# Strided q and k of two batches loaded in 96 rows of three pieces, batch 0's outputs placed behind its scores, and batch 1 in the order of the later batches

## The chip, the cores and the metric

The kernel runs on one core of one Trainium2 chip. The metric is the time of one execution on the device in microseconds (us); the figure that is compared is the median of several runs. A single profiled execution of each kernel supplies the spans, the waits and the order of the work.

## What is computed

Attention with two kinds of sparse mask over 8 batches, 8 heads, 576 positions and a head size of 64, then a two-layer block with a squared ReLU over the 4608 token rows. Heads 0 to 3 are *local* (a query sees itself and the 31 positions before it), heads 4 to 7 are *strided* (a query sees the earlier positions that are equal to it modulo 32).

```
scores = scale * q @ k.T                       # per batch and head
local:   0 <= i - j < 32
strided: i >= j and i % 32 == j % 32
attn = softmax(where(mask, scores, -1e9)); o = attn @ v
x = o.transpose(0, 2, 1, 3).reshape(4608, 512)
g = relu(x @ w_in) ** 2                        # 512 -> 2048
out = g @ w_out                                # 2048 -> 512
```

## The kernel before, in words

**Units.** A unit `u` is a pair of heads of one batch, four to a batch: units 0 and 1 of batch 0 are local, 2 and 3 strided, units 4 to 7 are batch 1, and so on. A unit goes through steps that are written as functions:

- T (`step_T`, L268 to L292): turns q or k so that the head size lies on the partitions. TensorE transposes slice by slice into one PSUM bank (L276) and ScalarE (L289) or VectorE (L291) copies 128x576 to SBUF. A local q or k takes six transposes of 96 rows, a strided one eight of 72 rows.
- S (`step_S`, L297 to L359): the scores, four half-tiles in four PSUM banks, one for each head of the pair and each half of the positions, matmuls at L325. For batch 0 a matmul (L313) first puts a mask bias in the bank; for later batches a mask is multiplied in afterwards by VectorE (L341). ScalarE takes the exponential of each bank (L335). With `at_once` the four exponentials stand together; otherwise they are spread over the next groups of the second stage (L354 to L359).
- N and O (`step_N`, `step_O`): only for the strided units of batch 0; row sums with a matrix of ones (L373), their inverse as exp(-ln) on ScalarE (L375, L376), the product with v (L386) and the scaling (L388).
- D (`step_D`): for all other units, attention times v in two or three parts (L410), each with a reciprocal and a multiplication on VectorE (L422, L423).
- E (`step_E`): the result is turned back (L440) and copied into `xt`, the input of the second stage (L446, L448).

**Second stage.** It walks over nine chunks of 512 rows. `mm1` (L464) makes one of 16 column blocks (`ff`) of the hidden layer with four matmuls of 512 columns, ScalarE applies ReLU (L470), VectorE squares (L473). `mm2` (L487) multiplies with `w_out`. These calls stand in a list of *groups*; attention steps are hooked in front of chosen groups. For batch 0, `first_steps` (L512 on) writes the order out by hand; beside each step stands the number of idle matmuls (`warm`, L502 to L506) that follow it. For batch 1 the calls of `second` (L731 to L748) name the group of each step; later batches come from `stream_steps` and are spread by weights.

**PSUM.** Eight banks: two `ph`, one `py`, five `pt`, each list taken in rotation. While `mm2` of chunk 0 runs, its fourth output holds one of the five `pt` banks.

**Queues.** Loads with a cast to bf16 are issued by GpSimd (POOL) in the order of the program: strided q and k of batch 0 (L226), local unit 1 (L130), v of batch 0, four parts of `w_in`, the first part of `w_out`, then in `loads_1` batch 1 mixed with the rest of `w_out`. The first local unit and, from batch 2 on, q, k and v come through SyncE (SP); the first of those waits for the last part of `w_out` (L117). TensorE, VectorE and ScalarE each run their instructions in the program's order.

**The strided loads.** `load_str_first` brings batch 0's strided q and k as 72 rows with 4 heads x 512 elements each into room in `w_out_b`; `load_qk_str` brings batch 1's unit by unit, again in 72 rows. From batch 2 on strided q and k are cast to DRAM and turned by the DMA queue, which leaves both strided units of a batch in one tile of 288 columns; `step_S` reads that layout where the batch is 2 or more (L322).

Of the kernel before, what the change touches and what calls it, by code (L numbers as in the profile page):

```python
# [14 lines left out]
def kernel(  # L15
# [125 lines left out]
                 s[name + "f"].rearrange("p h (j d) -> p h j d", j=6))  # L141
            s[name] = t

    def load_qk_str(u):
        b, p = units[u]
        s = st.setdefault(u, {})
        for name, src in (("q", q), ("k", k)):
            t = strT.tile([128, NJ // 2, 4 * SP_], BF16, name=f"{name}T_s")
            t = t.rearrange("p a c -> p (a c)")[0:SP_, 0:2 * NJ * D].rearrange("p (h c) -> p h c", h=2)
            nc.gpsimd.dma_start(out=t, in_=src[b, 2 * p:2 * p + 2]  # L150
                                .rearrange("h (p j) d -> p h (j d)", j=NJ))
            s[name] = t

    XB = 2
    big = {}
# [9 lines left out]
    def transpose_str(b):  # L165
        for name in "qk":
            o = strT.tile([128, NJ // 2, 4 * SP_], BF16, name=f"{name}T_s")
            nc.sync.dma_start_transpose(out=o, in_=big.pop((b, name)))
            for i in range(2):
                st.setdefault(4 * b + 2 + i, {})[name + "T"] = o[:, :, 2 * SP_ * i:2 * SP_ * (i + 1)]  # L170

    def transpose_local(u):
        s = st[u]
# [44 lines left out]
        for u in range(2):  # L218
            st.setdefault(4 * b + u, {})["v"] = vls[i + u]

    def load_str_first(names):
        for i, (name, src) in enumerate((("q", q), ("k", k))):
            if name not in names:
                continue
            t = w_out_b[0:SP_, 4 * i + 4:4 * i + 8, :]
            nc.gpsimd.dma_start(out=t, in_=src[0, 4:8].rearrange("h (p j) d -> p h (j d)", j=NJ))  # L226
            for u in (2, 3):
                st.setdefault(u, {})[name] = t[:, 2 * (u - 2):2 * (u - 1)]

    def load_v_str(u, eng):  # L230
        b, p = units[u]
        t = v_st.tile([SP_, 2, NJ * D], FP32, name="v_st")
# [35 lines left out]
    def step_T(u, name):  # L268
        s = st[u]
        local = is_local(u)  # L270
        n, w = (6, QL) if local else (NJ, SP_)
        src = s[name]
        src = src.rearrange("p j h d -> p (j h d)" if local else "p h c -> p (h c)")
        pt = bank("ph" if u < 4 else "pt").bitcast(BF16)[:, 0:S]
        for j in range(n):
            nc.tensor.transpose(pt[:, w * j:w * (j + 1)], src[:, 128 * j:128 * (j + 1)],  # L276
                                ident[0:w, 0:w])
        if local and name == "k":
            full = kTl[v_slot(u)]
            dst = full[:, 32:32 + S]  # L280
        else:
            full = dst = qkT.tile([128, S], BF16, name=f"{name}T")
        if local:
            o = dst.rearrange("c (p j) -> c p j", j=6)
            i = pt.rearrange("c (j p) -> c p j", j=6)
        else:
            o, i = dst, pt
        if name == "q" and (u > 3 or u == 0):
            nc.scalar.copy(o, i)  # L289
        else:  # L290
            nc.vector.tensor_copy(o, i)  # L291
        s[name + "T"] = full  # L292
# [4 lines left out]
    def step_S(u, at_once=False):  # L297
        s = st[u]
        qT, kT = s["qT"], s["kT"]
        local = is_local(u)  # L300
        w, n = (QL, NL) if local else (SP_, NJ)
        kn = 128 if local else SP_
        hn = n // 2
        e = es[u % 4]
        s["e"] = e
        pss = [[None, None], [None, None]]
        for half in range(2):
            for row in range(2):
                pss[row][half] = bank("pt")
                if u < 4:  # L310
                    bias = bias_l[:, half].rearrange("p t c -> p (t c)") if local \
                        else bias_s.rearrange("p t c -> p (t c)")
                    nc.tensor.matmul(pss[row][half][0:kn, 0:S // 2], ident[0:kn, 0:kn], bias,  # L313
                                     start=True, stop=False, skip_group_check=True)
            for i in range(hn):
                t = half * hn + i
                klo = w * t
                for row in range(2):
                    rows = slice(64 * row, 64 * row + 64)
                    if not local and units[u][0] >= XB:  # L320
                        c0 = w * (t // 4)
                        lhsT, rhs = (a[rows, t % 4, c0:c0 + w] for a in (kT, qT))  # L322
                    else:
                        lhsT, rhs = kT[rows, klo:klo + kn], qT[rows, w * t:w * (t + 1)]
                    nc.tensor.matmul(pss[row][half][0:kn, w * i:w * (i + 1)], lhsT, rhs,  # L325
                                     start=u > 3, stop=True, skip_group_check=u < 4)

        for row in range(2):
            for half in range(2):
                unread[id(pss[row][half])] = u  # L330

        def expo(row, half):
            del unread[id(pss[row][half])]
            lo = S * row + S // 2 * half
            nc.scalar.activation(e[0:kn, lo:lo + S // 2], pss[row][half][0:kn, 0:S // 2],  # L335
                                 AF.Exp, scale=scale)

        def masks(row):
            x = e[0:kn, S * row:S * (row + 1)].rearrange("p (t c) -> p t c", c=w)
            m = mask_full if local else mask_str.to_broadcast([kn, n, w])  # L340
            nc.vector.tensor_tensor(x, x, m, op=ALU.mult)  # L341

        if u < 4:
            for half in range(2):
                for row in range(2):
                    expo(row, half)
            return
        if at_once:
            for row in range(2):
                for half in range(2):  # L350
                    expo(row, half)
            later(1, lambda: masks(0), u)
            later(2, lambda: masks(1), u)
            return  # L354
        expo(0, 0)
        later(1, lambda: expo(0, 1), u)
        later(2, lambda: (masks(0), expo(1, 0)), u)
        later(3, lambda: expo(1, 1), u)
        later(4, lambda: masks(1), u)  # L359
# [146 lines left out]
                nc.tensor.matmul(pw, idle[:, 0:128], idle, start=True, stop=True)  # L506

    idle = xt[0][:, T - 512:T]
    first_order = (0, 2, 3, 1)
    NP = 5  # L510

    def first_steps():  # L512
# [3 lines left out]
        def part(kks, ffs=range(NP)):  # L516
            for ff in ffs:
                mm1(0, ff, kks, first_order, None if ff < 2 else "py" if ff == 2 else "pt")

        cast1 = lambda nm: (lambda: cast_qk_local(1, (nc.vector.tensor_copy,) * 2, nm))  # L520
        order = [(t(0, "q"), 2), (t(0, "k"), 3), (S_(0), 0), (t(2, "q"), 0), (t(2, "k"), 1), (S_(2), 0),
                 (t(3, "q"), 0), (t(3, "k"), 1), (cast1("q"), 0), (cast1("k"), 0), (S_(3), 0),
                 (t(1, "q"), 0), (t(1, "k"), 1), (D_(0, 0), 0), (D_(0, 1), 0), (n(2), 1), (S_(1), 1),
                 (o(2), 0), (E_(0), 0), (n(3), 0), (D_(1, 0), 0), (D_(1, 1), 0), (o(3), 0), (lambda: part((a, b)), 0),
                 (E_(1), 0), (lambda: part((c,)), 0), (lambda: part((d,)), 0)]
        return order

    def has_T(u):
        return units[u][0] < (LB if is_local(u) else XB)

    def stream_steps(lo, hi, base):
        order = [T_(lo, "q"), T_(lo, "k"), T_(lo + 1, "q"), S_(lo), T_(lo + 1, "k")]
# [22 lines left out]
    def loads_1():  # L555
        load_qk_local_sw(1, (4, 5), "q")
        load_qk_local_sw(1, (4, 5), "k")
        load_w_out(1)
        load_v_local_sw(1)
        load_qk_str(6)  # L560
        load_qk_str(7)
        load_v_str_sw(1)
        load_w_out(2)
        load_w_out(3)
        for t in vl_sts:
            nc.gpsimd.memset(t[0:32], 0.0)

    def loads(b):
# [6 lines left out]
        load_v_str(u + 3, nc.sync)  # L575
        if b >= XB:
            cast_str_dram(b)
        if b < XB:
            load_qk_str(u + 2)
        cast_qk_local(u, pool2)  # L580
        cast_qk_local(u + 1, pool2)
        if b < XB:
            load_qk_str(u + 3)
        cast_v_local(u)
        cast_v_local(u + 1)
        cast_v_str(u + 2)
# [18 lines left out]

    nc.scalar.preload_act_table_set("natural_log_exp_and_others")
    load_qk_local(0, nc.sync)
    load_str_first("qk")
    make_identity(nc, ident)
    nc.vector.memset(idle, 0.0)  # L610
    nc.vector.memset(mask_loc, 1.0)
# [45 lines left out]
    for fn, spare in first:  # L657
        fn()
        warm(spare)
        tick()  # L660
    late_constants()
    loads_1()

    NCH = T // 512
# [64 lines left out]

    dve2 = (nc.vector.tensor_copy,) * 2  # L730
    second(12, lambda: cast_qk_local(4, dve2))  # L731
    second(13, T_(4, "q"))
    second(14, T_(4, "k"), lambda: cast_qk_local(5, dve2))
    second(15, T_(5, "q"))
    second(16, S_(4, True), T_(5, "k"))
    second(18, S_(5, True))
    second(19, D_(4, 0), T_(6, "q"))
    second(20, D_(4, 1), T_(6, "k"), lambda: cast_v_str(6, nc.scalar.copy))
    second(21, S_(6, True), T_(7, "q"))
    second(22, E_(4), D_(5, 0), T_(7, "k"), lambda: cast_v_str(7, nc.scalar.copy))  # L740
    second(23, D_(5, 1), S_(7, True))
    second(24, D_(6, 0))
    second(25, E_(5), D_(6, 1))
    second(26, D_(6, 2))
    second(27, D_(7, 0))
    second(28, D_(7, 1), E_(6))
    second(29, D_(7, 2))
    second(31, E_(7))  # L748
    plan(2, 18, 0, 0)
    done_prev, g_prev = 0, 32  # L750
    plan(3, 34, 0, 0)
# [49 lines left out]
```

## Time and profile before

| | us |
|---|---|
| five runs | 324.71, 325.84, 319.21, 320.25, 321.17 |
| their median | 321.17 |
| the profiled execution | 324.71 |
| its span, first to last instruction | 322.7 |
| TensorE busy in the span | 303.5 |
| VectorE, ScalarE, GpSimd busy | 166.6, 163.9, 84.6 |

The profiled execution is near the top of the five. "PEclk" is the clock that was granted to TensorE, 1.00 being full speed; "idle before" is time that an engine sat still just before an instruction, with what ended it. TensorE carries the kernel: from 121 us to 305 us, 180.5 of 184 us are busy. Batch 0 takes the time from the start to about 30 us, batch 1 that from 38 us to 64.5 us; the first matmul of the second chunk starts at 64.53.

### The profile page before, as it was taken

The page shows a single profiled execution, that of the slowest core. Times are in us where ns is not written, and L with a number is a line of the kernel's source. Part 1 is how long each engine was busy: PE and PEld are TensorE (multiplying, and loading weights), DVE is VectorE, ACT ScalarE, POOL GpSimd, SP SyncE. Part 2 cuts the span into 40 slices and gives each one's busy share as a digit, 9 for nine tenths or more (in the row PEclk, how much of TensorE's full clock was granted, in tenths as well). Part 3 has the DMA queues.
Part 4 walks back from the last instruction along what each step waited for, and adds up shares of the span by engine and source line. Part 5 has one row for each costly group of instructions (what it writes and reads, how often), then busy time and mean ns, then how long its engine had stood idle before and what let it go on. Part 6 is the DMA issues. An engine that isn't in the chain of part 4 may idle for free.

```text
span 322.7 us, 6155 instructions
## 1 busy us (share of the span) xinstructions
PE 303.5 (94%) x2342; PEld 150.7 (47%) x2386; DVE 166.6 (52%) x408; ACT 163.9 (51%) x335; POOL 84.6 (26%) x108
## 2 busy tenths in 40 slices
PE   8699988999899998999999999999999999999995
PEld 3454445554455454444444444444454444444442
DVE  4444565547965786757575656565466222222200
ACT  3454666477554764554555455545553434434311
POOL 8542313714940623713084006000000000000000
PEclk9958999999999999999999999999999999999999
DMA  7999988899999998998699666000110110000121
GB/s 140 156 203 205 176 147 228 195 164 283 197 203 185 218 220 193 221 192 195 163 240 158 143 143 145 35 32 35 51 53 32 39 60 35 32 32 35 41 89 65
DMA packets 87949, 43.41 MB, mean 135 GB/s; under 512 B 72497, under 2 KB 81393, under 8 KB 87729
## 3 DMA queue, kind: packets, MB, share of 16 engines
q1 hardware_dynamic: 73520, 31.86, 42.7%
q0 software_dynamic: 14400, 11.17, 25.2%
q8 instruction: 18, 0.29, 0.4%
q14 instruction: 11, 0.08, 0.1%
HBM read 37.08 MB, written 12.98 MB: 155 GB/s over the span
## 4 chain that ended last, share of the span: by engine, by line
PE 84%; DVE 5%; DMA 3%; ACT 3%; issue 2%; POOL 2%; ACTq 0%; DVEq 0%; POOLq 0%
PE ph L464 35%; PE py L487 26%; PE ph L487 9%; PE pt L410 4%; PE pt L325 3%; DMA vl<-in_v_dram 3%; ACT r L470 2%; PE pt L440 2%; PE pt L276 1%; DVE xt L448 1%; PE pt L487 1%; DVE g_sb L473 1%; DVE x_l L423 1%; DVE e L341 1%; DVE kTl L291 1%
## 5 line engine op out<-in xcount | busy, mean ns | idle before, releaser
L464 PE MATMUL ph<-xt,w_in_b 128*128 128x512 bf16 x549 | 142.0, 380 | 3.4 <-DVE xt L448 1.9
L470 ACT ACTIVATE r<-ph 128x512 bf16<-128x512 f32 x141 | 84.0, 598 | 98.6 <-PE ph L464 94.1
L473 DVE TENSOR_TENSOR g_sb<-r 128x512 bf16<-128x512 bf16 x144 | 68.5, 478 | 109.2 <-ACT r L470 108.4
L487 PE MATMUL py<-w_out_b,g_sb 128*128 128x512 bf16 x381 | 99.9, 379 | 1.4 <-issue 0.5
L487 PEld LDWEIGHTS <-g_sb 128*128 128x128 bf16 x576 | 52.9, 98 | 60.0 <-issue 3.1
L464 PEld LDWEIGHTS <-w_in_b 128*128 128x128 bf16 x576 | 51.9, 98 | 54.8 <-issue 2.2
L335 ACT ACTIVATE e<-pt 128x288 bf16<-128x288 f32 (+1 forms) x128 | 48.3, 407 | 15.9 <-PE pt L325 15.7
L487 PE MATMUL ph<-w_out_b,g_sb 128*128 128x512 bf16 x152 | 37.1, 379 | 0.4
L410 PEld LDWEIGHTS <-e 72*128 72x128 bf16 (+1 forms) x416 | 22.4, 99 | 19.3 <-issue 2.7
L199 POOL CAST vl<-vl_st 128x768 bf16<-128x768 f32 x12 | 10.9, 911 | 49.6 <-DMA vl_st<-in_v_dram 42.6
L423 DVE TENSOR_TENSOR x_s<-pt,rinv 72x384 bf16<-72x384 f32 (+1 forms) x42 | 21.4, 509 | 1.4
L341 DVE TENSOR_TENSOR e<-e,mask_str 72x576 bf16<-72x576 bf16 x28 | 17.4, 621 | 3.9 <-ACT e L335 3.9
L140 POOL CAST q_l<-q_st 96x768 bf16<-96x768 f32 x12 | 11.8, 985 | 25.6 <-DMA q_st<-in_q_dram 13.8
L423 DVE TENSOR_TENSOR x_l<-pt,rinv 96x384 bf16<-96x384 f32 x32 | 17.7, 554 | 1.1
L422 DVE RECIPROCAL rinv<-pt 96x6 f32<-96x6 f32 (+2 forms) x74 | 13.6, 184 | 8.3 <-PE pt L410 8.1
L491 ACT COPY y<-py 128x512 f32<-128x512 f32 x25 | 14.7, 586 | 4.2 <-PE py L487 4.2
L410 PE MATMUL pt<-vs,e 72*128 72x65 bf16 x224 | 13.9, 193 | 1.2 <-ACT e L335 1.1
L341 DVE TENSOR_TENSOR e<-e,mask_full 128x576 bf16<-128x576 bf16 x28 | 14.2, 508 | 1.0 <-ACT e L335 1.0
L491 ACT COPY y<-ph 128x512 f32<-128x512 f32 x10 | 5.9, 586 | 17.0 <-PE ph L487 17.0
L140 POOL CAST k_l<-k_st 96x768 bf16<-96x768 f32 x12 | 11.0, 919 | 12.2 <-DMA k_st<-in_k_dram 12.1
L410 PE MATMUL pt<-vl,e 128*128 128x65 bf16 x192 | 11.3, 199 | 1.9 <-DMA vl<-in_v_dram 1.9
L240 POOL CAST vs<-v_st 72x1024 bf16<-72x1024 f32 x12 | 12.9, 1100 | 0.4
(101 smaller groups left out, 170.9 us busy)
## 6 DMA issues: line engine op xcount, KB each, us to landing
out_dram<-y SPq DMA_DIRECT2D x36, 256.0 KB, 2.0
vl_st<-in_v_dram SPq DMA_DIRECT2D x24, 144.0 KB, 4.0
v_st<-in_v_dram SPq DMA_DIRECT2D x12, 288.0 KB
q_st<-in_q_dram SPq DMA_DIRECT2D x16, 144.0 KB, 8.2
k_st<-in_k_dram SPq DMA_DIRECT2D x16, 144.0 KB, 5.7
w_in_b<-in_moe_w_in_dram POOLq DMA_DIRECT2D x4, 512.0 KB, 14.1
w_out_b<-in_moe_w_out_dram POOLq DMA_DIRECT2D x4, 512.0 KB, 13.3
q_d<-in_q_dram POOLq DMA_DIRECT2D x6, 288.0 KB, 5.1
```

The costliest lines, as they stand in the source:

```text
L140: copy(t.rearrange("p j h d -> p h j d"), s[name + "f"].rearrange("p h (j d) -> p h j d", j=6))
L240: (copy or nc.gpsimd.tensor_copy)(t[:, :, 0:D], s["vf"].rearrange("p h (j d) -> p (h j) d", d=D))
L335: nc.scalar.activation(e[0:kn, lo:lo + S // 2], pss[row][half][0:kn, 0:S // 2], AF.Exp, scale=scale)
L341: nc.vector.tensor_tensor(x, x, m, op=ALU.mult)
L410: nc.tensor.matmul(po[:, n - n0, :], e[0:kn, pos(n):pos(n) + 128], rhs[0:kn, src(n), 0:D + 1], start=True, stop=True)
L422: nc.vector.reciprocal(rinv[0:w, 0:m], po[0:w, 0:m, D:D + 1])
L423: nc.vector.tensor_tensor(x, po[0:w, 0:m, 0:D], rinv[0:w, 0:m].to_broadcast([w, m, D]), op=ALU.mult)
L464: nc.tensor.matmul(ph, w_in_b[:, kk, 128 * ff:128 * (ff + 1)], xt[kk][:, 512 * c:512 * (c + 1)], start=(kk == order[0]), stop=(kk == order ...
L470: nc.scalar.activation(r, ph, AF.Relu)
L473: later(1, lambda: nc.vector.tensor_tensor(g[:, ff, :], r, r, op=ALU.mult))
L487: nc.tensor.matmul(py, g[:, ff, 128 * j:128 * (j + 1)], w_out_b[:, ff, :], start=(ff == 0), stop=(ff == 15))
L491: nc.scalar.copy(y, py)
```

## The change

Five edits:

1. `load_str_first` and the old `load_qk_str` give way to one `load_qk_str` for batches 0 and 1. It brings the four strided heads as 288 rows of 512 elements, laid out as 96 partitions with 3 pieces; batch 0 into `w_out_b`, batch 1 into a `qk_st` buffer instead of `strT`.
2. `step_TS` turns them: for q or k two halves, each of six transposes of 96 rows into one bank, then one 128x576 copy, into the layout that the later batches use. `step_S` reads that layout for every strided unit.
3. Batch 0's order: both strided q halves ahead of the first scores, all scores ahead of row sums and outputs, other numbers of idle matmuls (ten after the first eight before, nineteen now), `late_constants` moved up onto VectorE behind the first k copy, and `mm1` taking the four parts of `xt` in their natural order.
4. Batch 1's order: a list in the manner of `stream_steps`, spread over groups 13 to 30; the scores of units 5 to 7 stay `at_once`, those of unit 4 do not.
5. `loads_1` has one call, two DMAs, where four DMAs stood.

```diff
-    def load_qk_str(u):
...
-            nc.gpsimd.dma_start(out=t, in_=src[b, 2 * p:2 * p + 2]
-                                .rearrange("h (p j) d -> p h (j d)", j=NJ))
+    def load_qk_str(b, names="qk", room=None):
...
+            if room is None:
+                t = qk_st.tile([QL, 2, 6 * D], FP32, name=f"{name}_st")
+                t = t.rearrange("p h c -> p (h c)").bitcast(BF16).rearrange("p (c x) -> p c x", c=3)
+            else:
+                t = room[0:QL, 3 * i:3 * i + 3, :]
+            nc.gpsimd.dma_start(out=t, in_=src[b, 4:8].rearrange("h (p j) d -> (h p) (j d)", j=NJ)
+                                .rearrange("(c r) x -> r c x", r=QL))
+            big[b, name] = t
...
+    def step_TS(b, name, half, copy):
+        if half == 0:
+            o = strT.tile([128, NJ // 2, 4 * SP_], BF16, name=f"{name}T_s")
+            for i in range(2):
+                st.setdefault(4 * b + 2 + i, {})[name + "T"] = o[:, :, 2 * SP_ * i:2 * SP_ * (i + 1)]
+            big[b, name + "T"] = o
+        src = big[b, name]
+        pt = bank("ph" if b == 0 else "pt").bitcast(BF16)[:, 0:S]
+        for j in range(2):
+            for c in range(3):
+                lo = 128 * (2 * half + j)
+                nc.tensor.transpose(pt[:, 3 * QL * j + QL * c:3 * QL * j + QL * (c + 1)],
+                                    src[:, c, lo:lo + 128], ident[0:QL, 0:QL])
+        copy(big[b, name + "T"][:, 2 * half:2 * half + 2, :].rearrange("c j p -> c (j p)"), pt)
...
-                    if not local and units[u][0] >= XB:
+                    if not local:
...
-    first_order = (0, 2, 3, 1)
+    first_order = (0, 1, 2, 3)
...
-        order = [(t(0, "q"), 2), (t(0, "k"), 3), (S_(0), 0), (t(2, "q"), 0), (t(2, "k"), 1), (S_(2), 0),
-                 (t(3, "q"), 0), (t(3, "k"), 1), (cast1("q"), 0), (cast1("k"), 0), (S_(3), 0),
-                 (t(1, "q"), 0), (t(1, "k"), 1), (D_(0, 0), 0), (D_(0, 1), 0), (n(2), 1), (S_(1), 1),
-                 (o(2), 0), (E_(0), 0), (n(3), 0), (D_(1, 0), 0), (D_(1, 1), 0), (o(3), 0), (lambda: part((a, b)), 0),
-                 (E_(1), 0), (lambda: part((c,)), 0), (lambda: part((d,)), 0)]
+        order = [(t(0, "q"), 2), (t(0, "k"), 0), (late_constants, 0), (ts("q", 0, s_), 0), (ts("q", 1, v_), 1), (S_(0), 1),
+                 (ts("k", 0, v_), 0), (ts("k", 1, v_), 2), (cast1("q"), 0), (cast1("k"), 0), (S_(2), 1),
+                 (t(1, "q"), 0), (t(1, "k"), 1), (S_(3), 3), (S_(1), 3), (n(2), 1), (n(3), 1),
+                 (D_(0, 0), 0), (D_(0, 1), 0), (D_(1, 0), 0), (D_(1, 1), 0), (o(2), 2), (E_(0), 1),
+                 (E_(1), 0), (o(3), 0), (lambda: part((a, b)), 0), (lambda: part((c,)), 0), (lambda: part((d,)), 0)]
...
-        load_qk_str(6)
-        load_qk_str(7)
+        load_qk_str(1)
...
-    second(13, T_(4, "q"))
-    second(14, T_(4, "k"), lambda: cast_qk_local(5, dve2))
-    second(15, T_(5, "q"))
-    second(16, S_(4, True), T_(5, "k"))
-    second(18, S_(5, True))
...
+    second(13, lambda: cast_qk_local(5, dve2))
+    second(22, lambda: cast_v_str(6, nc.scalar.copy))
+    second(24, lambda: cast_v_str(7, nc.scalar.copy))
+    ts = lambda nm, half: (lambda: step_TS(1, nm, half, nc.scalar.copy if nm == "q" else nc.vector.tensor_copy))
+    batch1 = [T_(4, "q"), T_(4, "k"), T_(5, "q"), S_(4), T_(5, "k"), S_(5, True), D_(4, 0), ts("q", 0), D_(4, 1),
+              ts("q", 1), ts("k", 0), D_(5, 0), ts("k", 1), E_(4), D_(5, 1), S_(6, True), E_(5), S_(7, True),
+              *D_all(6), D_(7, 0), E_(6), D_(7, 1), D_(7, 2), E_(7)]
+    for i, step in enumerate(batch1):
+        second(13 + i * 37 // (2 * len(batch1)), step)
```

## The prediction, made before the changed kernel was run

> **What bounds the kernel now.** I read the page's chain first, then the waits of TensorE in the part that the change touches, then the windows and the timeline of that part.
>
> The chain that ended last, by engine (page, part 4):
>
> ```profile
> PE 84%; DVE 5%; DMA 3%; ACT 3%; issue 2%; POOL 2%; ACTq 0%; DVEq 0%; POOLq 0%
> ```
>
> TensorE is the chain. Other engines count only where TensorE waits for them, so I price what the change does to TensorE's own work and to its waits before 64.53 us, where chunk 1 starts. Behind that point the order of all engines is the same in both kernels, PSUM bank numbers apart, and 180.5 of the 184 us from 121 to 305 are TensorE work: what is won or lost ahead of 64.53 moves the end one for one.
>
> TensorE's waits from 0 to 65 us (us in total, times, longest):
>
> ```profile
> PE pt L410 <- DMA vl<-in_v_dram: 1.9, 2, 1.4
> PE pt L276 <- DVE q_l L140: 1.7, 2, 1.2
> PE ph L276 <- DMA w_out_b<-in_k_dram: 1.4, 1, 1.4
> ...
> PE pt L325 <- DVE x_l L423: 0.7, 1, 0.7
> ```
>
> The change aims at these: v (1.9) and the strided k (1.4) in batch 0, q's cast (1.7) in batch 1. But a larger item is no wait. Windows (stretch, its length, busy us and instructions of PE, PEld, DVE, ACT, POOL, then clock, DMA share, GB/s):
>
> ```profile
> 6.09:9.50 3.41, 2.62 (x34) 1.38 (x32) 1.22 (x2) 1.50 (x5) 3.41 (x5) 1.00 1.22 175
> 9.50:12.92 3.42, 2.69 (x47) 1.84 (x48) 0.95 (x3) 1.33 (x4) 2.75 (x4) 1.00 2.19 165
> 12.92:16.33 3.41, 1.79 (x33) 1.19 (x33) 2.28 (x5) 1.33 (x4) 0.00 (x0) 1.00 1.77 134
> 16.33:19.74 3.41, 2.98 (x26) 1.44 (x27) 1.40 (x4) 1.40 (x3) 2.10 (x3) 0.50 1.23 201
> 19.74:23.15 3.41, 3.41 (x39) 1.71 (x40) 1.19 (x2) 2.11 (x6) 1.47 (x2) 0.50 1.24 207
> 23.15:26.57 3.42, 3.09 (x33) 1.87 (x33) 2.50 (x6) 1.25 (x3) 1.17 (x2) 0.50 1.24 206
> ```
>
> After a stretch with 1.79 us of TensorE work the clock is 0.50 for 10.24 us; stretches with 2.62 and 2.69 did not lower it.
>
> The timeline of TensorE around it (start, us, engine, line, operation):
>
> ```profile
> 6.18 0.42 PE L276 MATMUL ph<-ident,k_l 96*128 96x96 bf16 x6
> 6.44 0.81 PE L506 MATMUL py<-xt 128*128 128x512 bf16 x3
> 7.09 0.41 PE L313 MATMUL pt<-w_out_b,ident 128*128 128x288 bf16 x2
> ...
> 8.27 0.43 PE L276 MATMUL ph<-ident,w_out_b 72*128 72x72 bf16 x8
> 10.08 0.43 PE L276 MATMUL ph<-ident,w_out_b 72*128 72x72 bf16 x8 [1.38 <-DMA w_out_b<-in_k_dram]
> ...
> 16.30 0.23 PE L410 MATMUL pt<-vl,e 128*128 128x65 bf16 x1 [1.43 <-DMA vl<-in_v_dram]
> 16.96 0.65 PE L410 MATMUL pt<-vl,e 128*128 128x65 bf16 x9 [0.44 <-DMA vl<-in_v_dram]
> ```
>
> Strided q, issued at 1.43 and 6.8 us to landing, is there at 8.2; k (2.31 + 7.7) at 10.0; v at 16.9, where batch 0's outputs stand in front of the last scores.
>
> **What the Trainium skill says.** "TensorE: Matmul & The Clock Gate", § What's actually happening: a monitor looks at free-running windows of 3.41 us and lets half or all clock pulses through. The trace agrees: 10.24 us is three such windows, the values are 0.50 and 1.00. The same page, § Part 4: PE-mode transpose, says that transposes don't count as busy in the same way; the trace can't separate this. "DMA: Bandwidth & Descriptors", § Why a DMA increments its semaphore by 16 and not by 1: a DMA runs on the largest number of engines up to 16 that divides its slowest dimension. 72 rows give 12, 96 give 16. The views here don't list engines.
>
> **Part by part.**
>
> *The loads.* Both layouts move 288 rows of 512 elements. By the page 24 rows an engine become 18, a quarter less data time. That time is at most the 4.2 us from 4.0, where ScalarE gets the unit 0 rows that SP loaded ahead (its cast starts at 4.05), to q's landing at 8.2: a gain of 1.0 at most, and none at least. I take 0.6, an estimate for both: q at 7.6, k at 9.5.
>
> *The transposes.* Eight of 72 rows or six of 96: both follow each other every 0.26 us on TensorE (11.95 to 12.48 for two; 14.19 to 14.45 for one). Four stay four: nothing saved. Copies: a strided one takes 0.45 us on VectorE (L291), 0.64 on ScalarE (L289); four stay four.
>
> *Batch 0.* I set the new order out with the durations of the trace at full clock: scores 1.2 (10.57 to 11.95 less the wait for k), T 0.26, one idle matmul 0.22, the 12 of D 0.45, one N or O 0.35, exponential 0.33, D's VectorE part 0.70 (0.19 + 0.55 less overlap), O's scaling 0.63. TensorE finishes unit 0's k at 6.45 and now waits for q until 7.6: the new wait, 1.15. The engine is in order, so all scores stand behind it, and ScalarE's first exponential comes at about 9.0 instead of 7.79; the three idle matmuls that stood here have gone. Then q's halves to 8.2, S of unit 0 to 9.6, k's halves to 10.3 (k's wait is gone), two idle matmuls, S of unit 2 to 12.1 (behind k's copy at 11.15), T of unit 1 to 12.8, S of unit 3 to 14.3, S of unit 1 from 14.9 to 16.1, N of 2 and 3 to 17.7, D of both to 18.95 (v is there since 16.9: that wait is gone), O of 2 to 19.4. Now VectorE ends last: four D parts from 18.15 to 20.95, O's two scalings to 22.15; E of unit 1 goes to 21.3, its ScalarE copy to 22.1. The first second-stage group starts at 21.8 and stops for that copy; 20 matmuls of 0.216 end at 26.2, and the sixth column block starts there. In the trace it starts at 30.03. So **-3.8**. The nineteen idle matmuls are inside this: 17 after q cost 3.7 us of TensorE, mostly in place of waits.
>
> How much of the 3.8 is the clock? The old order, set out alike at full clock, starts that block at 26.3 (first group at 21.75 instead of 24.77, no slow matmuls). So nearly all of it: at equal clock the new order is worth 0.1. 324.71 - 3.7 = 321.0 for the old kernel at full clock, against the shown median of 321.17: the profiled run pays for the slow clock and the median run does not, or little.
>
> *Batch 1.* TensorE's idle in it, from the windows: 0.56 ahead of q of unit 4, then 7.62 - 6.39 = 1.2 (38.36 to 45.98) and 18.55 - 17.17 = 1.4 (to 64.53), 3.2 in sum. The new order keeps the first 0.6 (the cast still waits behind a square on VectorE) and removes the 1.2 at unit 5's q, whose cast now stands ahead of the k copy. It adds three waits. Unit 4's exponentials are no longer together: the second stands behind the ReLU of column block 15, and S of unit 5 needs the bank of the third. That ReLU ends 4.8 us after q of unit 4's transposes; two exponentials later, at 5.5, S can go on, while TensorE was free at 4.0: 1.4. S of unit 7 needs, with four banks left, the bank of E of unit 5, which ScalarE reads behind a 1.04 us copy of v (L240): 0.7. E of unit 7 stands straight behind the last part of D of unit 7: 0.19 + 0.42 on VectorE and two handovers, 0.9; before, 8 matmuls of 0.216 lay between. Sum 3.6 against 3.2: **+0.4**. If the bank waits are shorter than I count, -1.5; if a further one appears, +1.6.
>
> *Loads behind it.* Batch 1's strided DMAs move as many bytes, two issues of 0.7 us on POOL fewer; needed at about 41.9 (q) and 45.3 (k), where the old ones landed by 41.7 and 42.6. The buffers they take from `qk_st` are read by 47, before SP's loads for batch 2 may start (L117, at 48.17). `late_constants` covers 0.56 us of VectorE in the wait for q. **0**; without that cover at most 0.56.
>
> Sum: 324.71 - 3.8 + 0.4 = 321.3, from the profiled time (span 322.7 and 2.0 around it). Taking the middle of batch 1's bounds, which are about even around +0.1, I say **321.0**. That is the shown median.
>
> **Rivals.**
>
> *The clock falls at the new wait (slower).* From 6.09 to 9.50 TensorE now works 0.42 + 1.85 = 2.3 us, or 1.7 if q lands at 8.2; 1.79 lowered the clock, 2.62 did not. It decides somewhere between, and the windows lie differently in each run. Against it: the work afterwards is close-packed. Price: two or three windows at half clock. The trace's three cost 3.7; here, with ten idle matmuls of 0.43 instead of 0.22 among them, two cost 3.4 and three 5: 324.4 to 326.
>
> *Batch 1 flows and q is early (faster).* The three new waits fall to 1 us and k and q come 1.0 sooner: 321.3 - 2.6 - 0.4 = 318.3, 317.3 if the second stage's first groups also stop waiting for the last copy (1.0). For it: q's cast wait is the largest of the old list; against it: bank and ScalarE order are in the program.
>
> *The spread over 16 engines doesn't come (the loads don't do what they say).* q at 8.2: +0.6 on the dense stretch, 321.9.
>
> **How the numbers follow.** Main case 0.46, 319.3 to 323; third rival 0.08, 320 to 323.5, close to it; clock 0.21; batch 1 faster 0.25. A measurement of this kernel tells about 1% (3.2 us) from no change: faster means under 318.0, slower above 324.4. Faster: most of the last case, 0.20, and 0.03 of the main one. Slower: 0.17 of the clock case and 0.02 of the others. Same: 0.58. The range runs from 317.2 to 325.3.
>
> **What would show it.** Right: one TensorE wait of about 1.2 us for strided q near 6.5, none for k or v, clock 1.00 from 6 us on, the sixth column block at about 26.2, chunk 1 about 35 us later, and waits at unit 5's S (ScalarE) and unit 7's E (VectorE). Wrong: clock 0.50 somewhere from 8 us on (second case); chunk 1 before 59 us (third); or a wait for batch 1's strided loads, which I price at nothing.

## The result, and the profile after

| | before | after |
|---|---|---|
| median, us (executions) | 321.6 (80) | 323.39 (43) |
| lowest to highest | 318.37 to 330.4 | 320.79 to 328.72 |
| profiled execution, its span | 324.71, 322.7 | 322.19, 320.3 |

The ratio is 1.0075, 95% interval 1.0058 to 1.0092: slower by about 0.75%, 2.4 us. Ratios, here and below, leave out executions that took over 1.5% longer than the fastest of their kernel; the medians of all executions differ by 1.8 us. I had said 321.0, no change. The profiled executions alone would say the opposite, since that of before ran three windows at half clock and that of after none.

What follows turns on TensorE's clock. Each execution comes with its mean granted clock, and "full clock" means 0.997 or more here (in profiles of such executions the rest lies in the last microseconds of the program). Before is at full clock in 66 of the 168 executions that ran beside my experiments, after in 24 of 44. The medians of these are 319.7 and 322.0: at full clock the change costs 2.2 us.

The chain of work that ended last in after, by engine, is TensorE's still:

```profile
PE 86%; ACT 4%; DVE 4%; issue 2%; DMA 2%; ACTq 0%; DVEq 0%; POOLq 0%
```

TensorE's waits of after, 0 to 66 us (us in total, times, longest):

```profile
PE ph L186 <- DMA w_out_b<-in_q_dram: 1.5, 1, 1.5
...
PE pt L333 <- ACT e L343: 0.8, 1, 0.8
PE pt L448 <- DVE x_l L431: 0.7, 1, 0.7
PE pt L284 <- DVE q_l L140: 0.6, 1, 0.6
...
PE pt L448 <- DVE x_s L431: 0.5, 1, 0.5
PE pt L333 <- ACT xt L454: 0.3, 1, 0.3
```

The waits for v and k have gone, one for strided q has come (1.5, I had 1.15), and batch 1 has its new ones: S of unit 5 for the exponentials (0.8), S of unit 7 (0.3), E of unit 7 (0.5).

Windows of after (length, busy us and instructions of PE, PEld, DVE, ACT, POOL, clock, DMA share, GB/s):

```profile
7.16:10.57 3.41, 2.04 (x31) 1.34 (x33) 1.42 (x10) 1.43 (x4) 3.41 (x5) 1.00 1.52 171
...
16.33:19.74 3.41, 3.27 (x44) 1.61 (x43) 0.51 (x2) 3.11 (x9) 1.86 (x2) 1.00 1.23 204
19.74:23.15 3.41, 2.52 (x53) 1.68 (x52) 3.31 (x10) 2.01 (x4) 0.80 (x2) 1.00 1.24 206
```

In this execution the clock, which rose to full speed at 7.16, held through the wait for q. From 19.74 on VectorE is the busy engine (3.31 of 3.41 us); TensorE works 2.52. TensorE's timeline shows both waits, for q at 8.37 and for VectorE's `x_l` at 22.11 (start, us, operation, idle before):

```profile
8.37 0.68 PE L186 MATMUL ph<-ident,w_out_b 96*128 96x96 bf16 x12 [1.49 <-DMA w_out_b<-in_q_dram]
...
9.11 0.41 PE L321 MATMUL pt<-w_out_b,ident 128*128 128x288 bf16 x2
...
18.75 1.19 PE L418 MATMUL pt<-vl,e 128*128 128x65 bf16 x24
...
22.11 0.43 PE L448 MATMUL pt<-ident,x_l 96*128 96x96 bf16 x6 [0.73 <-DVE x_l L431]
22.47 0.51 PE L394 MATMUL pt<-e,g_sb 72*64 72x72 bf16 x16
22.91 1.16 PE L472 MATMUL ph<-xt,w_in_b 128*128 128x512 bf16 x4
...
27.36 1.89 PE L472 MATMUL ph<-xt,w_in_b 128*128 128x512 bf16 x8
```

q's transposes start at 8.37 (I had 7.6), the first scores at 9.11, the sixth column block at 27.36 (I had 26.2). Chunk 1 starts 34.77 later, at 62.13. This line of after, and the same of before:

```profile
62.13 1.89 PE L472 MATMUL ph<-xt,w_in_b 128*128 128x512 bf16 x8
64.37 1.89 PE L464 MATMUL ph<-xt,w_in_b 128*128 128x512 bf16 x8
```

(The 64.53 given for before further up stands in the list of its longest chain; all starts from here on are from TensorE's timeline.) To the end it is 320.3 - 62.13 = 258.2 us in after, and 322.7 - 64.37 = 258.3 in before: what is lost, is lost ahead of chunk 1.

### The profile page after: what moved, and what is told of

The parts are those of the page before. It is cut to its first block, busy times and chain, and to the rows that moved or that the text cites. A ratio compares the mean times of both kernels' runs of the same rounds, so it can differ in the third digit from the quotient of the medians.

```text
span 320.3 us, 6132 instructions
## 1 busy us (share of the span) xinstructions
PE 302.0 (94%) x2335; PEld 150.0 (47%) x2379; DVE 166.5 (52%) x407; ACT 164.2 (51%) x336; POOL 83.9 (26%) x106
## 4 chain that ended last, share of the span: by engine, by line
PE 86%; ACT 4%; DVE 4%; issue 2%; DMA 2%; ACTq 0%; DVEq 0%; POOLq 0%
PE ph L472 36%; PE py L495 27%; PE ph L495 10%; PE pt L333 4%; PE pt L418 4%; DMA w_out_b<-in_q_dram 2%; ACT r L478 1%; PE pt L448 1%; DVE xt L456 1%; ACT e L343 1%; PE pt L284 1%; PE pt L495 1%; PE py L514 1%; DVE g_sb L481 1%; PE pt L321 1%
## 5 line engine op out<-in xcount | busy, mean ns | idle before, releaser
L481 DVE TENSOR_TENSOR g_sb<-r 128x512 bf16<-128x512 bf16 x144 | 70.5, 491 | 106.0 <-ACT r L478 105.4
L418 PEld LDWEIGHTS <-e 72*128 72x128 bf16 (+1 forms) x416 | 21.8, 97 | 16.9 <-issue 1.9
L217 POOL CAST vl<-vl_st 128x768 bf16<-128x768 f32 x12 | 12.1, 1007 | 52.5 <-DMA vl_st<-in_v_dram 28.2
L430 DVE RECIPROCAL rinv<-pt 96x6 f32<-96x6 f32 (+2 forms) x74 | 13.6, 184 | 12.9 <-PE pt L418 11.2
L140 POOL CAST k_l<-k_st 96x768 bf16<-96x768 f32 x12 | 11.9, 991 | 13.9 <-DMA k_st<-in_k_dram 13.3
L140 POOL CAST q_l<-q_st 96x768 bf16<-96x768 f32 x12 | 10.6, 880 | 17.1 <-DMA q_st<-in_q_dram 17.0
L249 POOL CAST vs<-v_st 72x1024 bf16<-72x1024 f32 x12 | 13.6, 1163 | 1.2 <-DMA v_st<-in_v_dram 1.0
L349 DVE TENSOR_TENSOR e<-e,mask_full 128x576 bf16<-128x576 bf16 x28 | 12.7, 454 | 0.4 <-ACT e L343 0.3
L514 PE MATMUL py<-xt 128*128 128x512 bf16 x24 | 9.4, 486 | 1.6 <-DVE xt L615 1.3
```

Source lines behind the costliest of these rows:

```text
L140: copy(t.rearrange("p j h d -> p h j d"), s[name + "f"].rearrange("p h (j d) -> p h j d", j=6))
L249: (copy or nc.gpsimd.tensor_copy)(t[:, :, 0:D], s["vf"].rearrange("p h (j d) -> p (h j) d", d=D))
L418: nc.tensor.matmul(po[:, n - n0, :], e[0:kn, pos(n):pos(n) + 128], rhs[0:kn, src(n), 0:D + 1], start=True, stop=True)
L430: nc.vector.reciprocal(rinv[0:w, 0:m], po[0:w, 0:m, D:D + 1])
L481: later(1, lambda: nc.vector.tensor_tensor(g[:, ff, :], r, r, op=ALU.mult))
```

## Experiments

Theory A: batch 0's order costs, as it is longer at equal clock. Its parts: A1, all scores stand behind the late q; A2, the outputs behind all scores leave VectorE's D and O parts to the end; A3, the idle matmuls lie on the path. Rival B: only the clock, which falls at the new wait. Rival C: batch 1's order.

| kernel | median (executions) | ratio, interval | at full clock: executions, median | sixth block, chunk 1 in its profile |
|---|---|---|---|---|
| before, all executions | 321.4 (168) | | 66, 319.7 | |
| after | 323.39 (43) | 1.0075, 1.0058 to 1.0092 | 24 of 44, 322.0 | 27.36, 62.13 |
| c_before | 321.54 (1) | | 0 | 26.89, 61.01 |
| b0_only | 323.71 (15) | 1.0093, 1.0062 to 1.0125 | 3, 321.9 | 26.99, 61.23 |
| b1_only | 321.81 (22) | 1.003, 1.0003 to 1.0058 | 12, 320.8 | 26.82, 62.78 |
| gap_filled | 322.22 (15) | 1.0069, 1.0043 to 1.0094 | 15, 322.2 | 26.88, 61.66 |
| before_filled | 321.11 (22) | 1.0006, 0.9982 to 1.003 | 22, 321.1 | 26.16, 60.27 |
| s0_first | 322.51 (20) | 1.0061, 1.0038 to 1.0084 | 20, 322.5 | 26.82, 61.59 |
| old_order | 320.35 (14) | 0.9993, 0.9956 to 1.003 | 10, 319.6 | 26.10, 60.87 |
| no_fill | 325.29 (6) | 1.015, 1.0105 to 1.0196 | 0 | 29.55, 64.45 |
| s0_first_no_idle | 323.4 (22) | 1.0076, 1.0045 to 1.0108 | 0 | 28.27, 63.06 |
| old_order_old_b1 | 318.64 (18) | 0.9947, 0.9925 to 0.9969 | 16, 318.6 | 24.90, 59.19 |
| before_few_idle | 319.83 (22) | 0.9961, 0.994 to 0.9983 | 22, 319.8 | 25.18, 60.17 |
| outputs_last | 321.38 (14) | 1.0, 0.997 to 1.0031 | 4, 319.7 | 26.44, 60.71 |

**c_before**, the kernel before, unchanged.

> The kernel before, unchanged, for a profile of an execution whose clock stays at 1.00. Theory A (the loss sits in batch 0's order): the sixth column block starts near 25.6 us, chunk 1 near 60.1, 34.5 us between them. Theory C (the loss sits in batch 1's order): the sixth block starts near 27.4 as in the changed kernel and chunk 1 near 60.1.

Its clock was 0.50 from 12.01 to 18.84, two windows, so it doesn't show the old order at full clock, which it was run for. But its time, 321.54, is near the median of before: the median execution of before also pays for a slow clock.

**b0_only and b1_only**, one batch each in the new manner. For b0_only the old per-unit load and the old calls of `second` come back; for b1_only the old first load, order and `first_order`:

```diff
# b0_only
-        load_qk_str(1)
+        load_qk_str_unit(6)
+        load_qk_str_unit(7)
...
-    second(13, lambda: cast_qk_local(5, dve2))
+    second(13, T_(4, "q"))
# b1_only
-    load_qk_str(0, room=w_out_b[:, 4:10, :])
+    load_str_first("qk")
...
-    first_order = (0, 1, 2, 3)
+    first_order = (0, 2, 3, 1)
```

> Batch 0 as changed (loads, transposes, order), batch 1 as before. Theory A: nearly the whole loss, ratio to before 1.005 to 1.007. Theory B (only the clock): the same ratio, but no loss in the executions whose clock stays at 1.00. Theory C: ratio 1.000 to 1.002.

> Batch 1 as changed, batch 0 as before. Theory A and B: +0.3 us as the two profiles show from the sixth column block to chunk 1 (34.77 against 34.50), ratio 1.000 to 1.002. Theory C: ratio 1.005 or more.

Batch 0 alone gives the whole loss: 1.0093, and at full clock, in three executions, 321.9 against 319.7. Batch 1 alone gives 0.3%, at full clock 1.1 us. C is not the main cause.

**gap_filled**, eight idle matmuls in the wait for q:

```diff
-        order = [(t(0, "q"), 2), (t(0, "k"), 0), (late_constants, 0), (ts("q", 0, s_), 0), (ts("q", 1, v_), 1), (S_(0), 1),
+        order = [(t(0, "q"), 2), (t(0, "k"), 8), (late_constants, 0), (ts("q", 0, s_), 0), (ts("q", 1, v_), 1), (S_(0), 1),
```

> The changed kernel with eight idle matmuls in the wait for strided q, nothing else. Theory B: the clock stays at 1.00 in all executions and the median falls by the whole loss, to 320.5 to 321.5. Theory A: the clock stays at 1.00, the spread of the executions shrinks, but the median only falls from 323.4 to about 321.9, the level of the changed kernel's executions at full clock.

All 15 executions are at full clock, and the median falls by 1.2 us; 0.7% of loss stays. So B is a part of after's time, and not the loss against before, which pays for its own clock as well.

**before_filled**, the old order with its waits filled:

```diff
-        order = [(t(0, "q"), 2), (t(0, "k"), 3), (S_(0), 0), (t(2, "q"), 0), (t(2, "k"), 1), (S_(2), 0),
+        order = [(t(0, "q"), 2), (t(0, "k"), 3), (S_(0), 0), (t(2, "q"), 6), (t(2, "k"), 1), (S_(2), 0),
...
-                 (t(1, "q"), 0), (t(1, "k"), 1), (D_(0, 0), 0), (D_(0, 1), 0), (n(2), 1), (S_(1), 1),
+                 (t(1, "q"), 0), (t(1, "k"), 8), (D_(0, 0), 0), (D_(0, 1), 0), (n(2), 1), (S_(1), 1),
```

> The kernel before, with five matmuls on the idle tile more in its wait for strided k (six after unit 2's q) and seven more in its wait for v (eight instead of one after unit 1's k). Nothing of the change is in it. It shows the old order at full clock, which no profile so far does. Theory A (at equal clock the old order of batch 0 is about 1.5 to 2 us shorter than the new one, from what undisturbed executions of it take): the clock stays at 1.00, the sixth column block starts at 25.0 to 25.8, the median is 319 to 320, below the kernel before by about 0.5% and with a narrower spread. Rival (my forecast: at equal clock both orders start that block at 26.2 to 26.3): block at 26.3 or later, median 320.5 to 321.5.

The clock held, and the time didn't fall: the median, 321.1, is what the text above expects if my forecast is right, and the block, at 26.16, lies between what it expects from theory A and from my forecast. But the idle matmuls behind unit 1's k end at 16.4, and D could have started at 15.2. before_few_idle, below, has five idle matmuls fewer there and is otherwise the same: its block comes 0.98 us earlier, its median is 1.3 lower, and all executions of both are at full clock. Five take 5 x 0.22 = 1.1 us. Filled beyond its wait, the clock's gain is given back.

**s0_first**, A1's test:

```diff
-        order = [(t(0, "q"), 2), (t(0, "k"), 0), (late_constants, 0), (ts("q", 0, s_), 0), (ts("q", 1, v_), 1), (S_(0), 1),
+        order = [(t(0, "q"), 2), (t(0, "k"), 3), (late_constants, 0), (S_(0), 0), (ts("q", 0, s_), 0), (ts("q", 1, v_), 1),
```

> The kernel after, with the scores of unit 0 put ahead of strided q's transposes (and three idle matmuls after unit 0's k again), so that ScalarE's first exponential doesn't wait for q. Theory A1 (the loss is that all scores stand behind the late q: 1.2 us of TensorE work could be done in that wait): first exponential at about 7.8 instead of 9.4, sixth block at about 26.0 instead of 26.9 to 27.4, no clock drop in the wait, median 1.2 to 1.8 below the kernel after, 321.6 to 322.2. Theory A2 (outputs behind all scores leave VectorE's D and O parts last): they end as late as before, since VectorE is not what the scores free up; block moves by less than 0.4, median within 0.7 of gap_filled's 322.2. Theory A3 (17 idle matmuls on the path): the same as A2 here.

Scores at 7.4 instead of 9.1, and the block at 26.82 against gap_filled's 26.88, the median 322.5 against 322.2. A1 falls: what is won at the front does not reach the block.

**old_order**, the new loads and transposes in batch 0's old order, which goes on behind these lines as in the kernel before:

```diff
+        order = [(t(0, "q"), 2), (t(0, "k"), 3), (S_(0), 0), (ts("q", 0, s_), 0), (ts("q", 1, v_), 0),
+                 (ts("k", 0, v_), 0), (ts("k", 1, v_), 1), (S_(2), 0),
+                 (cast1("q"), 0), (cast1("k"), 0), (S_(3), 0),
...
```

> The new loads (96 rows) and the wider transposes of batch 0, but in the old order of the steps: unit 0's scores ahead of q, outputs of units 2 and 0 between the scores, late constants behind the first steps as before; batch 1 as in the kernel after. Theory A2 (the new order of outputs is what costs): about as the kernel before plus batch 1's 0.5, or 321.8 to 322.1, with the sixth block at about 25.5 if the clock holds and 26.5 to 27 if it falls in the wait for k. Theory A1: the same as A2 here, since unit 0's scores stand ahead again. Rival (the loads or the transposes themselves cost, not the order): 323 or more.

At full clock 319.6 (10 executions) against 322.0 for after: the new order of batch 0, its idle matmuls included, costs 2.3 us. The loads and transposes are not the loss. The median is below all that I had expected of this run.

**no_fill** and **s0_first_no_idle**: after and s0_first without idle matmuls behind q's transposes (each number there set to 0).

> The kernel after, without the idle matmuls behind strided q's transposes (17 of 0.22 us, 3.7 in all, less those that lie in waits). Theory A3 (they stand on the path): sixth block about 1 us earlier, median about 1 us below the kernel after where the clock holds. Theory A1 and A2: their place is taken by waits for the exponentials and for D's parts, the block doesn't move by more than 0.4 at full clock, and TensorE's clock falls in more of the executions, so the median is equal or 0.5 to 2 us above.

> The kernel after, with unit 0's scores ahead of strided q (as in s0_first, 322.5) and no idle matmul behind that (the outputs stay behind all scores). Theory A3: sixth block at 24.5 to 25.4, median 319.8 to 320.6, about as the old order. Theory A1 together with A3 (each gives a part): 0.5 to 1 below wait_fill_only. Theory A2 (VectorE's parts, which start behind all scores, set the end): sixth block at 26.2 to 26.8, with waits of TensorE for D's and O's parts on VectorE of 1.5 us or more, median 321.5 to 322.5.

Neither was at full clock in any execution. In the profiles (0.971 and 0.979) the clock stays down for five and four windows: that is what the idle matmuls of the new order prevent, and in the median it costs more than they do. But seven of the 22 executions of s0_first_no_idle lost only one window (clock 0.992 to 0.995). Their median is 321.4, which is 1.1 below s0_first at full clock (322.5), though a slow window is in it, and 2.3 below the fifteen executions of after with the same clock (323.7). So the idle matmuls do stand on the path (A3), at a cost of more than 1.1 us.

**old_order_old_b1 and before_few_idle**, the old order at full clock with few idle matmuls, with the new loads and with the old ones:

```diff
# old_order_old_b1: old_order with batch 1 as before, and
-        order = [(t(0, "q"), 2), (t(0, "k"), 3), (S_(0), 0), (ts("q", 0, s_), 0), (ts("q", 1, v_), 0),
+        order = [(t(0, "q"), 2), (t(0, "k"), 3), (S_(0), 0), (ts("q", 0, s_), 0), (ts("q", 1, v_), 4),
# before_few_idle: before_filled, and
-                 (t(1, "q"), 0), (t(1, "k"), 8), (D_(0, 0), 0), (D_(0, 1), 0), (n(2), 1), (S_(1), 1),
+                 (t(1, "q"), 0), (t(1, "k"), 3), (D_(0, 0), 0), (D_(0, 1), 0), (n(2), 1), (S_(1), 1),
```

> Batch 0's new loads and wider transposes in the old order of steps, with four idle matmuls in what is left of the wait for k; batch 1 as in the kernel before. My reading (the order of batch 0 costs about 2 us, the new batch 1 about 0.5, the loads and transposes gain a little, and the clock costs what falls): clock 1.00, sixth block at 24.5 to 25.2, chunk 1 about 34.2 later, median 318.5 to 319.4, faster than the kernel before by 0.6 to 0.9%, of which the clock is about 0.6. If the wider transposes and loads are worth nothing beyond the clock, as before_few_idle, 319.4 to 320.

> The kernel before, with five idle matmuls more in its wait for strided k and two more (three instead of one) in its wait for v; before_filled had seven more there and they ended 1.1 us behind v. Theory (the full clock alone is worth 1.5 to 2 us to the median of the kernel before, and v lands at about 15.3 in most executions): sixth block at 25.0 to 25.4 with the clock at 1.00, median 319.4 to 320, no execution above 322. Rival (my forecast's old order at full clock, block at 26.3): median 320.5 or more. If the clock still falls at the wait for v in a part of the executions, the spread to 325 stays.

Both beat before and after; old_order_old_b1 is the best kernel here, by 0.5% over before (0.3 to 0.8). The two differ in batch 0's loads and transposes and in five idle matmuls (13 against 18). TensorE in before_few_idle:

```profile
14.56 0.81 PE L506 MATMUL py<-xt 128*128 128x512 bf16 x3
15.21 0.68 PE L410 MATMUL pt<-vl,e 128*128 128x65 bf16 x12
...
20.59 1.04 PE L464 MATMUL ph<-xt,w_in_b 128*128 128x512 bf16 x4
...
25.18 1.89 PE L464 MATMUL ph<-xt,w_in_b 128*128 128x512 bf16 x8
```

Three idle matmuls fill the wait for v; D starts at 15.21, without a wait. In the profile that I worked from most of it started at 16.96: v landed at 16.9 there and at 15.4 here. At full clock, then, the old order starts the block at 25.2, not at 26.3.

**outputs_last**, A2's test: old_order_old_b1, with the outputs behind all scores as in after:

```diff
-                 (ts("k", 0, v_), 0), (ts("k", 1, v_), 1), (S_(2), 0),
-                 (cast1("q"), 0), (cast1("k"), 0), (S_(3), 0),
-                 (t(1, "q"), 0), (t(1, "k"), 1), (D_(0, 0), 0), (D_(0, 1), 0), (n(2), 1), (S_(1), 1),
-                 (o(2), 0), (E_(0), 0), (n(3), 0), (D_(1, 0), 0), (D_(1, 1), 0), (o(3), 0), (lambda: part((a, b)), 0),
-                 (E_(1), 0), (lambda: part((c,)), 0), (lambda: part((d,)), 0)]
+                 (ts("k", 0, v_), 0), (ts("k", 1, v_), 1), (cast1("q"), 0), (cast1("k"), 0), (S_(2), 0),
+                 (t(1, "q"), 0), (t(1, "k"), 1), (S_(3), 0), (S_(1), 1), (n(2), 1), (n(3), 0),
+                 (D_(0, 0), 0), (D_(0, 1), 0), (D_(1, 0), 0), (D_(1, 1), 0), (o(2), 0), (E_(0), 0),
+                 (E_(1), 0), (o(3), 0), (lambda: part((a, b)), 0), (lambda: part((c,)), 0), (lambda: part((d,)), 0)]
```

(and `first_order` (0, 1, 2, 3)). Both have 13 idle matmuls.

> The kernel old_order_old_b1 (318.6; sixth block at 24.90, first second-stage group at 20.32) with its loads, its idle matmuls and its place of unit 0's scores, and with one thing changed: the outputs of batch 0 stand behind all scores, in the order of the kernel after. Theory A2 (outputs behind all scores leave VectorE's D and O parts, 5 us one behind the other, to the end): first group 1 us or more later, sixth block at 25.9 to 26.6, median 319.6 to 320.4, with a wait of TensorE for x_l on VectorE. Theory A3 (the idle matmuls of the kernel after are the loss, its order isn't): sixth block at 24.7 to 25.4, median 318.4 to 319.1.

Up by 2.7 us in the median; 1.1 at full clock, though only 4 of 14 executions are. Its TensorE:

```profile
17.56 0.34 PE L429 MATMUL pt<-vl,e 128*128 128x65 bf16 x6 [0.41 <-ACT g_sb L394]
...
18.42 0.43 PE L459 MATMUL pt<-ident,x_l 96*128 96x96 bf16 x6
19.80 0.51 PE L459 MATMUL pt<-ident,x_l 96*128 96x96 bf16 x6 [0.95 <-DVE x_l L442]
20.25 0.69 PE L405 MATMUL pt<-e,g_sb 72*64 72x72 bf16 x16
```

and the windows around it:

```profile
16.59:20.01 3.42, 1.95 (x51) 1.54 (x49) 2.98 (x9) 2.55 (x5) 1.19 (x1) 1.00 1.24 206
20.01:23.42 3.41, 3.41 (x29) 1.54 (x26) 2.00 (x4) 0.64 (x1) 1.28 (x2) 0.50 1.24 206
```

Though TensorE took q up 0.4 us earlier here (8.29 against 8.71), E of unit 1 waits for VectorE, TensorE works 1.95 of 3.42 us, and the clock falls just before the second stage begins. The cause lies in VectorE's timeline, first of old_order_old_b1:

```profile
15.56 0.19 DVE L441 RECIPROCAL rinv<-pt 96x6 f32<-96x6 f32 x1
...
16.48 0.55 DVE L442 TENSOR_TENSOR x_l<-pt,rinv 96x384 bf16<-96x384 f32 x1
18.41 1.20 DVE L407 TENSOR_TENSOR xt<-pt,g_sb 128x288 bf16<-128x288 f32 x2 [1.38 <-PE pt L405]
19.52 0.18 DVE L441 RECIPROCAL rinv<-pt 96x6 f32<-96x6 f32 x1
...
20.91 1.18 DVE L407 TENSOR_TENSOR xt<-pt,g_sb 128x288 bf16<-128x288 f32 x2
```

and of after:

```profile
19.20 0.19 DVE L430 RECIPROCAL rinv<-pt 96x6 f32<-96x6 f32 x1 [4.38 <-PE pt L418]
...
21.50 0.55 DVE L431 TENSOR_TENSOR x_l<-pt,rinv 96x384 bf16<-96x384 f32 x1
21.97 2.29 DVE L396 TENSOR_TENSOR xt<-pt,g_sb 128x288 bf16<-128x288 f32 x4
```

In the old order two of the four D parts are done by 17.0, under scores and outputs. In the new one VectorE sits idle for 4.38 us and then has four D parts and all of O's scalings one behind the other, 5.1 us, and TensorE waits 0.73 us in it (0.95 in outputs_last). So A2's mechanism is shown. Its size is less sure. The 1.1 rests on four executions. The two kernels also ran on different chips, and at full clock before took 320.4 beside outputs_last (7 executions) and 319.7 beside the other (23): held against these, the difference is 0.4. In the profiles TensorE goes from k's halves to the first group of the second stage in 11.2 us against 10.2, a part of it at the slow clock.

**The sum at full clock.** The medians form a chain: before_few_idle 319.8, old_order_old_b1 318.6 (-1.2), outputs_last 319.7 (+1.1), s0_first 322.5 (+2.8); after, which A1 alone sets apart from s0_first, has 322.0. Each step is a difference of two medians, so that the end comes out right proves nothing. The +2.8 holds the new batch 1 and the idle matmuls, of which s0_first has 15 behind k's halves and outputs_last 4. From k's halves to D, first in s0_first and then in outputs_last:

```profile
9.96 0.67 PE L186 MATMUL ph<-ident,w_out_b 96*128 96x96 bf16 x12 [0.73 <-ACT qT_s L188]
...
18.21 1.19 PE L418 MATMUL pt<-vl,e 128*128 128x65 bf16 x24
...
9.70 0.67 PE L196 MATMUL ph<-ident,w_out_b 96*128 96x96 bf16 x12
...
16.43 0.72 PE L429 MATMUL pt<-vl,e 128*128 128x65 bf16 x18
```

That is 8.25 against 6.73 us, 1.5 more, with eight idle matmuls more (8 x 0.22, about 1.7); the other three stand behind D, where TensorE waits for VectorE in any case. Batch 1 takes 0.5 more by the profiles (below). The rest of the 2.8, 0.8, I can't place. So at full clock the loss is made of idle matmuls on the path (about 1.5), outputs last (0.4 to 1.1) and a smaller part of batch 1. The kernel that would have measured A3 alone at full clock, with eight idle matmuls in the wait for q and none behind (the `wait_fill_only` of an expectation above), gave no result: that A3 costs is shown, its size is worked out.

## Why the prediction was wrong, point by point

**The step that failed** is "The old order, set out alike at full clock, starts that block at 26.3 [...] So nearly all of it: at equal clock the new order is worth 0.1." It starts at 25.2, idle matmuls included (before_few_idle): I had built v's landing in one profile, 16.9, into it, where D starts at 15.2 otherwise. The new order's own end, 26.2, was too early in turn: it came at 27.4 in after and at 26.9 with the wait for q filled. So at equal clock the new order costs 1.7 to 2.2 us and gains nothing.

**The baseline** hid this: "the profiled run pays for the slow clock and the median run does not, or little". Before is at full clock in 66 of 168 executions, 319.7 in the median; the others have 323.1. The five shown times, 319.21 and 320.25 beside 324.71 and 325.84, could have warned me that 321.17 is no full-clock time. My sum, 321.3, is near what after takes at full clock (322.0); what it was held against was 1.5 too high.

**The loads.** "q at 7.6": in the nine profiles with the new loads it landed at 7.6 to 8.7, in the five with the old ones at 7.7 to 8.4, with a median of 8.2 in both. No gain for q, as in my third rival, but not for that rival's reason. I cited the Trainium skill, "DMA: Bandwidth & Descriptors", § Why a DMA increments its semaphore by 16 and not by 1, for a spread over 16 engines in place of 12; that it names an exception for some copies issued by GpSimd, I left out. The traces agree with 12 and 16. A load reports its landing in 16 counts: in before four of q's come at 4.6 to 4.9 and twelve at 6.3 to 8.2, in after all sixteen at 5.6 to 8.3 (that the first four stand for engines without a share is my reading). Thirteen are there by 6.9 in after, but TensorE needs the last. What stands behind q did gain: k landed at 9.1 to 10.1 (9.8 to 10.0 with the old loads), and batch 0's local v at 13.6 to 15.1 (15.3 to 16.9). In after TensorE takes q up 0.8 later than I had it, two thirds of the 1.2 by which 27.36 misses 26.2.

**The transposes**, "nothing saved": right. The 24 of 96 rows take 1.04 us of TensorE in old_order_old_b1, and so do the 32 of 72 rows in before_few_idle. From k's first transposes to unit 1's q it is 3.48 us in the first (10.17 to 13.65) and 4.10 in the second (9.94 to 14.04), since unit 3's q is turned ahead of k now (0.26), one idle matmul has gone (0.22) and with it a wait for k's copy (0.19). Most of the 1.2 us between these kernels lies elsewhere. In their profiles it is 1.1: 0.3 up to the block, 0.7 from there to chunk 1, where in before_few_idle ScalarE waits for batch 1's strided v until 45.0 (43.6 in the other) and TensorE behind it 1.2 us for exponentials in place of 0.4. Whether v's landing there has to do with the loads, one profile of each can't tell.

**Batch 0's VectorE end** was set out rightly ("Now VectorE ends last", E of unit 1 waiting for it), except that O's scalings are four of 0.57 us, not two of 0.6: VectorE ended at 24.3, not 22.15. What its late end costs didn't show in my result, since the old order that I held it against was wrong. The idle matmuls I called "inside this", "mostly in place of waits"; between k's halves and D they are not (1.5 us for eight, above).

**The clock rival** (0.21) came true in 20 of 44 executions of after, at 2.2 us (324.2 against 322.0), mostly for one window, where I had priced two or three. gap_filled, with the wait for q filled, has no such execution, so the wait is where it comes from. It isn't what makes after slower, as before loses no less (323.1 against 319.7, in 102 of 168).

**Batch 1**, +0.4: right in size, with luck in its parts. Block to chunk 1 takes 34.8 to 34.9 in six of the seven kernels with the new batch 1, 34.1 to 34.3 in six of the seven with the old one (b1_only has 36.0 and before_few_idle 35.0). The three waits are where I put them, but shorter: 0.8 and 0.2, 0.3, 0.5, in all 1.8 where I had 3.0. TensorE's whole idle time in the stretch is nevertheless 3.6 us in after, against 3.4 in old_order_old_b1. In the medians at full clock the new batch 1 costs 1.1 (b1_only against before), 1.0 (old_order against old_order_old_b1) or 0.1 (after against b0_only, three executions). The rival "batch 1 flows" had a slip of its own: three waits of 3.0 that fall to 1 give 2.0, not 2.6.

**Behind chunk 1**, 0: right (258.2 and 258.3). Twelve of the fourteen profiles have 257.8 to 258.6 there; s0_first and outputs_last have 259.9 and 260.0, nearly all of it between chunks 1 and 2, where all kernels run the same steps. That spread I can't explain.

## What to carry to other kernels

Before you compare two orders, bring both to the same clock and to several executions' landings: three slow windows (3.4 us) and one late transfer (1.1 us of the block), built into one side, were worth more than the whole change (2.2). An engine that idles early and ends last (here VectorE, 4.4 us idle, then 5.1 packed) is a reason to keep its work spread between the scores, even where TensorE looks well packed. Idle matmuls hold the clock at no cost only inside a wait that is there anyway; five behind its end cost 1.0 us (before_filled against before_few_idle), about their full 0.22 each.

## What the hardware showed that I had not expected

**The busy time of a window doesn't settle the clock.** I had put the point of decision between 1.79 and 2.62 us of TensorE work. In old_order:

```profile
8.96:12.38 3.42, 2.61 (x42) 1.70 (x43) 2.04 (x5) 1.37 (x5) 3.16 (x5) 1.00 1.99 151
12.38:15.79 3.41, 3.19 (x44) 2.47 (x43) 1.52 (x4) 1.65 (x5) 1.35 (x2) 0.50 1.27 206
```

2.61 lowered it, and 2.04 in after, from 7.16 to 10.57, did not. The transposes, which the Trainium skill says don't count in the same way ("TensorE: Matmul & The Clock Gate", § Part 4: PE-mode transpose), don't explain that: they are 0.68 of the 2.61 and 0.76 of the 2.04, so without them too the kernel that did less kept its clock. What does count stays open. That the windows run freely (same page, § What's actually happening) fits: one kernel has full clock in some executions and not in others.

**A VectorE copy beside a GpSimd memset took about three times as long.** In b1_only:

```profile
34.19 1.43 POOL L585 MEMSET vl_st<- 32x768 f32 x2
...
34.74 1.09 DVE L140 COPY q_l<-q_st 96x768 bf16<-96x768 bf16 x1
35.76 0.34 DVE L140 COPY k_l<-k_st 96x768 bf16<-96x768 bf16 x1
```

1.09 us beside the memset, 0.34 behind it, and TensorE waited 1.29 us for it. In after the memset runs 1.2 us earlier and the same copy takes 0.35. Two more profiles show it: a copy that starts with the memset takes 0.96 in b0_only and 0.97 in outputs_last. No experiment was made on it.
